# The hidden layer of an MLP in groups of four 128-column blocks instead of two, behind a top-k attention

## The chip, the cores and the metric

The kernel runs on one core of a Trainium2 chip. The time is the device time of one execution in microseconds (us), the median over runs; lower is better. Five engines work side by side, each through its own queue in order: TensorE (PE in the profile; its weight loads are PEld), VectorE (DVE), ScalarE (ACT), GpSimd (POOL), and SyncE (SP), which issues the DMAs.

## The reference

```python
# top-k attention, q, k, v: (8, 8, 576, 64) float32, top_k = 32
scores = scale * np.matmul(q, k.transpose(0, 1, 3, 2))
kth = np.partition(scores, -top_k, axis=-1)[..., -top_k:-top_k + 1]
scores = np.where(scores >= kth, scores, -1000000000.0)
scores = scores - np.max(scores, axis=-1, keepdims=True)
attn = np.exp(scores)
attn = attn / (np.sum(attn, axis=-1, keepdims=True) + 1e-09)
x = np.matmul(attn, v)          # then (B, H, S, D) -> (4608, 512)
# MLP, w_in: (512, 2048), w_out: (2048, 512)
h = x @ w_in
g = np.where(h >= 1, h, np.where(h <= -1, 0.0, (h + 1) ** 2 / 4))
out = g @ w_out
```

The kernel computes g as min(relu(0.5 h + 0.5), 1) squared, plus relu(h - 1).

## The kernel before, in words

**Attention.** The work is cut into 144 steps. A step m is one tile of 128 query rows (of one of 8 batches) for a pair of heads. A step consists of:

- `scores` (L285, L287): PE writes the scores `sp` of 128x576 for each of two heads into PSUM, and ACT copies them to `s`.
- `first_top` (L300 to L323): DVE makes `more`, the pairwise maximum of two halves of the scores, and the first eight maxima; ACT takes `nmax` and the exponentials `e` of both heads. DVE's L300 also makes `less`, the pairwise minimum, for the step before.
- `weights` (L348 to L386): DVE finds the 32 largest with rounds of eight maxima and a match_replace, then the threshold `kth`, and L386 masks `e` and sums it to `z`.
- `divide` (L332, L339, L342): DVE takes 1/z as `rz`; POOL multiplies `e` by it, one instruction a head, and records `excess`, a number for a check at the end.
- `move_w` (L416 to L419): ACT splits `e` into 16-bit `halves`, one instruction a head; SP writes them to DRAM as `rows` and fetches them back transposed as `wT`.
- `values` (L433, L441, L446): PE multiplies `wT` with the values into `po`, and ACT copies this into the tile's `xT`.

DVE's loop over a step is long, so the stages of several steps are interleaved. With step m running on DVE, the scores of step m+2 and the values of step m-2 are issued at slot 4 of seven; the division of step m-1 stands at slot 0 and its `halves` at slot 2.

**MLP.** Four steps complete one chunk of 128 tokens, 36 chunks in all. `mlp` then queues that chunk's work. `hidden(x)` multiplies `w_in` with `xT` for GROUP = 2 blocks of 128 hidden columns into one PSUM tile `ph` (L466). ACT reads it twice (L470 gives `r`, L477 gives `g`), and POOL finishes with a clamp, a square and a sum (L482, L483, L484). `final(f)` accumulates block f times `w_out` into `py` (L489), and after the 16th block ACT copies `py` to `y` and SP stores it. A final comes LAG = 4 groups behind its hidden group. The last chunk uses groups of one block and lets DVE and ACT do POOL's part.

**Order.** Nothing reorders at run time: the order of each engine's instructions is written down by the builder. `mlp` appends to `pending`, first in first out; `advance` runs after each of the seven slots and takes units off while their cost (128-column passes of PE: `NK * group` for a hidden group, four for a final) fits the amount that is due by then. The amount is spread evenly over the remaining steps. Every instruction of a unit, on PE, ACT and POOL, enters the engines' order at that point:

```python
pending.append((NK * group, needed(x * group + group - 1, False), partial(hidden, x), False))
...
if due < cost or pe_time >= until:
    break
```

**Early stage.** In the first 13 or so steps the two weight matrices arrive as 64 pieces of 64-bit words and are converted by ACT, DVE and POOL (`convert_piece`). A hidden group can be queued only when all its blocks' pieces are there. In this stage the division and the transpose of `e` are done by PE (`transpose_w`) instead of POOL, `halves` and DMA. From then on, every second step ACT also runs two `sign` instructions (L168) that inspect a weight piece.

**PSUM and SBUF.** `ph` and `po` share three PSUM banks; `sp`, `pq`, `pk` and `pw` share two double banks; `py` has one. `r` has 2 buffers, `g` has 2 * LAG, `y` has 2.

Of the kernel before, what the change touches and what calls it, by code (L numbers as in the profile page):

```python
# [10 lines left out]
F32 = mybir.dt.float32  # L11
# [4 lines left out]
ALU = mybir.AluOpType  # L16
# [8 lines left out]
def kernel(  # L25
# [10 lines left out]
    nc = tc.nc  # L36
    B, H, S, D = q.shape
    NTOK, DM = out.shape
    DFF = moe_w_in.shape[1]
    P = 128  # L40
# [10 lines left out]
    BANK = 512  # L51
    NK = DM // P
    NF = DFF // P
    GROUP = 2
    LAG = 4
    SCALE = float(D) ** -0.5

    const = ctx.enter_context(tc.tile_pool(name="const", bufs=1))
# [42 lines left out]
    n_pieces = NK * DFF // WC + NF * DM // WC  # L101
# [12 lines left out]
    def needed(f, second):  # L114

        return (f // n_in) * (NK + n_in * n_out) + NK + (n_out * (f % n_in + 1) if second else 0)
# [55 lines left out]
    def run(ctx, paired):  # L172
# [284 lines left out]
        def mlp(xT, rows, pool, last):  # L457
            gs, group = {}, 1 if last else GROUP
            py = []

            def hidden(x):
                ph = ps.tile([P, group, P], F32, name="ph", tag="ph", bufs=3)
                for i in range(group):
                    f = x * group + i
                    for kk in range(NK):
                        nc.tensor.matmul(ph[:, i], w_in[:, kk, f * P:(f + 1) * P], xT[:, kk],  # L466
                                         start=(kk == 0), stop=(kk == NK - 1))

                r = pool.tile([P, GROUP, P], F32, name="r", bufs=2)[:, 0:group]
                nc.scalar.activation(r, ph, AF.Relu, bias=half, scale=0.5)  # L470
                gs[x] = g = pool.tile([P, GROUP, P], F32, name="g", bufs=2 * LAG)[:, 0:group]
                if last:
                    nc.vector.tensor_scalar(g, ph, -1.0, 0.0, ALU.add, ALU.max)
                    nc.scalar.activation(r, r, AF.Square)
                    nc.vector.scalar_tensor_tensor(out=g, in0=r, scalar=1.0, in1=g, op0=ALU.min, op1=ALU.add)
                    return
                nc.scalar.activation(g, ph, AF.Relu, bias=minus, scale=1.0)  # L477
                if converted < n_pieces and x % 2:
                    nc.scalar.activation(r, r, AF.Square)
                    nc.gpsimd.tensor_scalar(r, r, 1.0, 0.0, ALU.min, ALU.max)  # L480
                else:
                    nc.gpsimd.tensor_scalar(r, r, 1.0, 0.0, ALU.min, ALU.max)  # L482
                    nc.gpsimd.tensor_tensor(out=r, in0=r, in1=r, op=ALU.mult)  # L483
                nc.gpsimd.tensor_tensor(out=g, in0=r, in1=g, op=ALU.add)  # L484

            def final(f):
                if f == 0:
                    py.append(ps.tile([P, DM], F32, name="py", tag="py", bufs=1))
                nc.tensor.matmul(py[0], gs[f // group][:, f % group], w_out[:, f, :], start=(f == 0), stop=(f == NF - 1))  # L489
                if f == NF - 1:  # L490
                    y = (late or words).tile([P, DM], F32, name="y", bufs=2)
                    nc.scalar.copy(y, py[0])  # L492
                    for p0, p1, dst in rows:
                        nc.sync.dma_start(out=dst, in_=y[p0:p1])

            behind = []
            while pending and pending[-1][3]:
                behind.insert(0, pending.pop())  # L500
            for x in range(NF // group + LAG):
                if x < NF // group:
                    pending.append((NK * group, needed(x * group + group - 1, False), partial(hidden, x), False))
                if x < LAG:
                    for _ in range(min(GROUP, len(behind))):
                        pending.append(behind.pop(0)[0:3] + (False,))
                else:
                    for f in range((x - LAG) * group, (x - LAG + 1) * group):
                        pending.append((DM // P, needed(f, True), partial(final, f), x >= NF // group))
# [3 lines left out]
        for b in range(0, B, 2):  # L513
            a, c, tl = [(b, t) for t in range(NT)], [(b + 1, t) for t in range(NT)], (b, NT)
# [15 lines left out]
        words, late = conversion.enter_context(tc.tile_pool(name="words", bufs=1)), None  # L530
        pending = deque()
        total, spent = len(chunks) * (NK * NF + NF * DM // P), 0
        converted, inspected, due = 0, 0, 0.0
# [127 lines left out]
        for m in range(n + 2):  # L661
# [3 lines left out]
            elif not early and late is None:  # L665
                conversion.close()
                late = ctx.enter_context(tc.tile_pool(name="late", bufs=1))
# [108 lines left out]
```

## Time and profile before

| what | us |
|---|---|
| runs (3): lowest, median, highest | 1607.3, 1609.65, 1610.31 |
| the profiled execution, its own time | 1610.32 |
| its span in the trace | 1608.5 |
| PE busy | 1514.0 (94%) |
| DVE busy | 1422.1 (88%) |
| ACT busy | 1140.4 (71%) |
| POOL busy | 943.3 (59%) |
| ACT reading `ph`: L470 and L477, 280 each of 128x256 | 133.1 and 131.8 |
| POOL's L482, L483, L484 | 150.7, 201.5, 219.6 |

Times in the profile are in us from the span's start. A row of the timeline gives start, duration, engine, source line, operation, the tiles written and read, shapes and a count; a bracket at its end gives the engine's idle time before it and what ended that. A row of the waits gives the waiting instruction, what it waited for, the total, the number of times and the longest. PE's ends are modelled, so PE's busy time is an upper estimate of what it did.

### The profile page before, as it was taken

Reading aid. Unit: us, or ns where it says so; the run is one execution under the profiler, and the core shown is the slowest. Engines: PE = TensorE matmul, PEld = TensorE weight load, DVE = VectorE, ACT = ScalarE, POOL = GpSimd, SP = SyncE. Lnnn points to the kernel's source line nnn. Section 1 sums busy time; section 2 is a strip of 40 time slices with the busy share of each in tenths; the row PEclk is TensorE's granted clock in tenths of the full one; section 3 lists DMA queues with packets and bytes.
Section 4 is the critical chain, followed back from the end, with each engine's and each line's share of the span. In section 5 each row is a group of like instructions: output and inputs, shape, how many; then the busy total and the mean of one; then the engine's idle time right before and its main releaser. Section 6 shows DMA issues by size and latency. Waiting matters only on the chain.

```text
span 1608.5 us, 32395 instructions
## 1 busy us (share of the span) xinstructions
PE 1514.0 (94%) x10925; PEld 1080.7 (67%) x10925; DVE 1422.1 (88%) x4443; ACT 1140.4 (71%) x2308; POOL 943.3 (59%) x1376
## 2 busy tenths in 40 slices
PE   5587999999999999999999999999999999999988
PEld 4465676777667776777667767766666667666665
DVE  7999889999998998999999998999898998889932
ACT  5677567777777767777768877776677776677632
POOL 5766466666555665655556666555555665556640
PEclk7798999999999999999999999999999999999999
DMA  9433246565465556665565545655565555544410
GB/s 252 132 96 110 72 130 174 157 158 153 133 174 161 154 143 173 161 150 145 145 172 159 160 133 157 172 143 140 135 174 146 142 142 130 145 131 126 123 51 16
DMA packets 439056, 227.92 MB, mean 142 GB/s; under 512 B 393056, under 2 KB 401248, under 8 KB 438880
## 3 DMA queue, kind: packets, MB, share of 16 engines
q1 hardware_dynamic: 438880, 225.75, 51.8%
q8 instruction: 88, 1.44, 0.4%
q14 instruction: 88, 0.72, 0.1%
HBM read 62.91 MB, written 86.11 MB: 93 GB/s over the span
## 4 chain that ended last, share of the span: by engine, by line
PE 71%; ACT 13%; POOL 4%; DVE 4%; DMA 4%; issue 3%; SPq 1%; POOLq 0%; ACTq 0%; DVEq 0%
PE ph L466 27%; PE py L489 24%; PE sp L285 8%; PE po L433 7%; ACT halves L416 3%; ACT e L323 3%; DMA wT<-rows 2%; ACT s L287 2%; ACT sign L168 2%; PE pw L401 1%; POOL e L339 1%; POOL r L483 1%; PE po L441 1%; ACT r L470 1%; POOL g L484 1%
## 5 line engine op out<-in xcount | busy, mean ns | idle before, releaser
L466 PEld LDWEIGHTS ph<-xT,w_in 128*128 128x128 f32 x4608 | 554.4, 192 | 118.3 <-issue 79.8
L466 PE MATMUL ph<-xT,w_in 128*128 128x128 f32 x4608 | 576.1, 278 | 14.8 <-ACT xT L446 12.9
L489 PE MATMUL py<-w_out,g 128*128 128x512 f32 x1152 | 558.6, 601 | 7.3 <-ACT y L492 7.1
L482 POOL TENSOR_SCALAR r<-r 128x256 f32<-128x256 f32 x276 | 150.7, 546 | 526.5 <-ACT r L470 526.1
L307 DVE MATCH_REPLACE8 more<-tops,more 128x288 f32<-128x288 f32 x864 | 375.2, 437 | 0.0
L416 ACT COPY halves<-e 128x1152 uint16<-128x1152 uint16 x260 | 288.0, 1153 | 112.7 <-POOL e L339 111.5
L470 ACT ACTIVATE r<-ph,half 128x256 f32<-128x256 f32 (+1 forms) x296 | 139.0, 470 | 241.1 <-PE ph L466 227.9
L489 PEld LDWEIGHTS py<-w_out,g 128*128 128x128 f32 x1152 | 193.5, 191 | 137.0 <-issue 131.2
L386 DVE SCALAR_TENSOR_TENSOR e<-s,kth,e 128x577 f32<-128x577 f32 x288 | 249.2, 900 | 0.1
L484 POOL TENSOR_TENSOR g<-r,g 128x256 f32<-128x256 f32 x280 | 219.6, 784 | 22.0
L323 ACT ACTIVATE e<-s,nmax 128x576 f32<-128x576 f32 x288 | 217.4, 770 | 4.7
L339 POOL TENSOR_SCALAR e<-e,rz 128x576 f32<-128x576 f32 x260 | 218.6, 851 | 0.0
L483 POOL TENSOR_TENSOR r<-r 128x256 f32<-128x256 f32 x276 | 201.5, 730 | 23.0
L300 DVE TENSOR_TENSOR more<-s 128x576 f32<-128x576 f32 x144 | 114.9, 798 | 109.0 <-ACT s L287 108.6
L287 ACT ACTIVATE s<-sp 128x576 f32<-128x576 f32 x288 | 169.2, 638 | 4.5 <-PE sp L285 4.2
L285 PE MATMUL sp<-kT,qT 64*128 64x288 f32 x1024 | 162.0, 433 | 9.9 <-ACT kT L244 9.0
L285 PEld LDWEIGHTS sp<-kT,qT 64*128 64x128 f32 x1024 | 89.6, 188 | 98.9 <-issue 29.1
L433 PE MATMUL po<-wT,v_in 128*64 128x128 f32 x2048 | 145.9, 282 | 10.3 <-DMA wT<-rows 7.9
L433 PEld LDWEIGHTS po<-wT,v_in 128*64 128x64 f32 x2048 | 113.4, 139 | 60.5 <-issue 37.5
L477 ACT ACTIVATE g<-ph,minus 128x256 f32<-128x256 f32 x280 | 131.8, 471 | 0.0
L348 DVE MAX8 tops<-more 128x8 f32<-128x288 f32 x288 | 125.4, 442 | 0.0
L300 DVE TENSOR_TENSOR less<-s 128x576 f32<-128x576 f32 x144 | 117.4, 815 | 0.0
(92 smaller groups left out, 1528.2 us busy)
## 6 DMA issues: line engine op xcount, KB each, us to landing
rows<-halves SPq DMA_DIRECT2D x130, 576.0 KB, 2.8
raw<-in_moe_w_out_dram SPq DMA_DIRECT2D x52, 256.0 KB, 2.8
raw<-in_moe_w_in_dram SPq DMA_DIRECT2D x48, 256.0 KB, 2.9
k_in<-in_k_dram SPq DMA_DIRECT2D x64, 128.0 KB, 3.2
q_in<-in_q_dram SPq DMA_DIRECT2D x32, 256.0 KB, 3.3
v_in<-in_v_dram SPq DMA_DIRECT2D x8, 1024.0 KB, 5.9
out_dram<-y SPq DMA_DIRECT2D x32, 256.0 KB, 3.0
kT<-in_moe_w_in_dram SPq DMA_DIRECT2D x16, 256.0 KB, 4.6
```

Of the source, the lines that this page charges most:

```text
L285: nc.tensor.matmul(o[:, a0 - c0:a1 - c0], qT[d, g, :], kT[d, g, k0:k0 + a1 - a0], start=True, stop=True)
L300: nc.vector.tensor_tensor(out=x, in0=s[:, :, 0:SH], in1=s[:, :, SH:S], op=op)
L307: nc.vector.match_replace(out=st["rest"][:, i, :], in_to_replace=eight(st["tops"], i, r - 8), in_values=src[:, i, :], imm_value=LOWEST)
L323: nc.scalar.activation(e[:, i, :], s[:, i, :], AF.Exp, bias=nmax[:, i:i + 1])
L339: nc.gpsimd.tensor_scalar(st["e"][:, i, :], st["e"][:, i, :], rz[:, i:i + 1], 1.0, ALU.mult, ALU.mult)
L386: nc.vector.scalar_tensor_tensor(out=st["all"][1][:, i, :], in0=st["all"][0][:, i, :], scalar=last[i], in1=st["all"][1][:, i, :], op0=ALU. ...
L416: nc.scalar.copy(halves[:, :, i * S:(i + 1) * S], st["e"][:, i, :].bitcast(U16).rearrange("p (k t) -> p t k", t=2))
L433: nc.tensor.matmul(po[j * D:(j + 1) * D], v_in[:, h, c, :] if c < NT else v_tl[0][:, h, :], wT[:, block(j, c)], start=(c == 0), stop=(c == ...
L466: nc.tensor.matmul(ph[:, i], w_in[:, kk, f * P:(f + 1) * P], xT[:, kk], start=(kk == 0), stop=(kk == NK - 1))
L483: nc.gpsimd.tensor_tensor(out=r, in0=r, in1=r, op=ALU.mult)
L484: nc.gpsimd.tensor_tensor(out=g, in0=r, in1=g, op=ALU.add)
L489: nc.tensor.matmul(py[0], gs[f // group][:, f % group], w_out[:, f, :], start=(f == 0), stop=(f == NF - 1))
```

## The change

GROUP becomes 4 and LAG becomes 2, so the distance between a block's hidden and final products stays eight blocks for all chunks but the last, where groups are of one block and the distance falls from four blocks to two. `ph` then fills a whole PSUM bank with 128x512. ACT reads it with two instructions of 512 columns. POOL's three operations stay at 256 columns: they are issued for the first two blocks, then for the last two. The cost that `advance` compares with the due amount is `NK * group`, so a hidden unit costs 16 instead of 8 and is taken off half as often. `r` grows with GROUP; `g` keeps its size (half as many buffers, twice as large); `y` has one buffer instead of two.

```diff
-    GROUP = 2
-    LAG = 4
+    GROUP = 4
+    LAG = 2
...
                 nc.scalar.activation(g, ph, AF.Relu, bias=minus, scale=1.0)
-                if converted < n_pieces and x % 2:
+                squared = converted < n_pieces and x % 2
+                if squared:
                     nc.scalar.activation(r, r, AF.Square)
-                    nc.gpsimd.tensor_scalar(r, r, 1.0, 0.0, ALU.min, ALU.max)
-                else:
-                    nc.gpsimd.tensor_scalar(r, r, 1.0, 0.0, ALU.min, ALU.max)
-                    nc.gpsimd.tensor_tensor(out=r, in0=r, in1=r, op=ALU.mult)
-                nc.gpsimd.tensor_tensor(out=g, in0=r, in1=g, op=ALU.add)
+                for c in range(0, group, 2):
+                    rh, gh = r[:, c:c + 2], g[:, c:c + 2]
+                    nc.gpsimd.tensor_scalar(rh, rh, 1.0, 0.0, ALU.min, ALU.max)
+                    if not squared:
+                        nc.gpsimd.tensor_tensor(out=rh, in0=rh, in1=rh, op=ALU.mult)
+                    nc.gpsimd.tensor_tensor(out=gh, in0=rh, in1=gh, op=ALU.add)
...
-                    y = (late or words).tile([P, DM], F32, name="y", bufs=2)
+                    y = (late or words).tile([P, DM], F32, name="y", bufs=1)
```

## The prediction, made before the changed kernel had run

> **What bounds the kernel now.** I read the page's busy shares first, then the total waits, then one step of the timeline on ACT and on POOL, and last the order of instructions in the two built programs, which holds no times.
>
> ```profile
> PE 1514.0 (94%) x10925; PEld 1080.7 (67%) x10925; DVE 1422.1 (88%) x4443; ACT 1140.4 (71%) x2308; POOL 943.3 (59%) x1376
> POOL r L482 <- ACT r L470: 526.1, 201, 9.0
> ACT r L470 <- PE ph L466: 227.9, 155, 3.5
> ACT halves L416 <- POOL e L339: 111.5, 59, 3.5
> DVE more L300 <- ACT s L287: 108.6, 89, 4.9
> ```
>
> PE is nearly full, and its few stalls after 200 us add up to about 30 us (it waits for `xT` 14.8, for `wT` some 10, for `y` 7.1). By the shares, ACT and POOL have room to spare. The waits say otherwise: ACT waits for POOL's `e`, and POOL waits for ACT's `r`. That is a ring. ACT's queue runs `halves` of one step, then everything up to `r`; POOL's queue runs the three operations on `r`, then `e`; and `e` releases the next `halves`. Here is one turn on ACT, then the part on POOL that closes it:
>
> ```profile
> 778.46 2.21 ACT L416 COPY halves<-e 128x1152 uint16<-128x1152 uint16 x2 [2.80 <-POOL e L339]
> 780.57 0.47 ACT L470 ACTIVATE r<-ph,half 128x256 f32<-128x256 f32 x1
> 780.94 0.46 ACT L477 ACTIVATE g<-ph,minus 128x256 f32<-128x256 f32 x1
> 781.29 0.20 ACT L321 ACTIVATE nmax<-tops 128x2 f32<-128x2 f32 x1
> 781.52 1.44 ACT L323 ACTIVATE e<-s,nmax 128x576 f32<-128x576 f32 x2
> 782.87 1.17 ACT L287 ACTIVATE s<-sp 128x576 f32<-128x576 f32 x2
> 783.93 0.26 ACT L446 COPY xT<-po 128x128 f32<-128x128 f32 x1
> 784.08 0.49 ACT L470 ACTIVATE r<-ph,half 128x256 f32<-128x256 f32 x1
> 784.45 0.49 ACT L477 ACTIVATE g<-ph,minus 128x256 f32<-128x256 f32 x1
> 788.17 2.21 ACT L416 COPY halves<-e 128x1152 uint16<-128x1152 uint16 x2 [3.23 <-POOL e L339]
> ```
>
> ```profile
> 784.67 1.24 POOL L482 TENSOR_SCALAR r<-r 128x256 f32<-128x256 f32 x1 [1.63 <-ACT r L470]
> 785.99 0.61 POOL L483 TENSOR_TENSOR r<-r 128x256 f32<-128x256 f32 x1
> 786.68 0.72 POOL L484 TENSOR_TENSOR g<-r,g 128x256 f32<-128x256 f32 x1
> 787.38 1.50 POOL L339 TENSOR_SCALAR e<-e,rz 128x576 f32<-128x576 f32 x2
> ```
>
> In this turn neither `r` waits for PE. The time from `halves` to `halves`, 9.71 us, is the sum of the queue: ACT 5.62 to the second `r`, 0.59 until POOL starts, 2.71 for three operations, 0.79 for the first `e`. The next turn, which holds the two `sign` instructions, takes 10.45 us (778.46, 788.17, 798.62). PE's work in such a step is 9.62 us (scores at 777.46 and at 787.08). So PE and the ring run almost level. The mean over all 129 turns of the trace is 10.40 us.
>
> **ScalarE's two reads.** 280 instructions of 475 ns and 280 of 471 ns become 140 pairs of 512 columns. No such row exists; the ACT copy `y` of 128x512 from PSUM takes 587 ns, and the line through `r` at 128 columns (367) and 256 (475) gives 690. I take 0.6, nearest to the copy. ACT's busy time falls by 265 - 280 x 0.6 = 97 us. That is worth nothing by itself: in the ring only what stands before `r`'s end counts, and there one early pair of `r` and `g` goes (0.72 us in the turn shown) and the remaining `r` grows by 0.13.
>
> **GpSimd: the same operations, at another place.** Count and size stay. What moves is which of them stand between `r` and `e`. Before, each turn holds two hidden groups. One has its three operations done while ACT is at `e` and `s`; only the other is in the ring. Now each turn holds one group of four blocks, all six operations come from one `r`, and where that `r` is the last thing before `halves`, all six stand ahead of `e`. I matched POOL's order with ACT's in the changed program, for each of 129 turns: are all POOL operations of the hidden groups that ACT has read before `halves` queued ahead of this `halves`' `e`, and does ACT read `ph` after `s`? Both hold in 66 turns (35 without `sign`, 31 with), mostly in three stretches of about 20. In 30 turns POOL's six are ahead, but ACT reads `ph` early, among `nmax` and `e`; in 33 the six are queued behind `e`. Those 63 leave the ring slack.
>
> **The sum for a tight turn.** ACT from `halves` to `r`: 5.62 - 0.72 = 4.90. From `r` to POOL's start 0.57 (mean where POOL was idle), plus 0.13 for the wider read: 0.70. POOL's three operations ahead of an `e` take 2.24 us on the mean of 128 (1.88 to 3.19), twice: 4.48. `e` until `halves` starts: 0.88 (mean; 0.79 above). Total 10.96 us, with `sign` 1.17 more (791.92 to 793.09): 12.13. So 35 x 10.96 + 31 x 12.13 = 760 us where 66 x 10.40 = 686 stood: **+74 us**. Bounds: six operations at the least seen, 2 x 1.88, with 0.66 and 0.78 at their ends, give +17; at the 2.71 of the turn above they give +126. I stay at the mean, because one POOL group will meet DVE's two-input L300 (the 1.24 above, against 0.40 elsewhere) and the other will not: 2.71 + 1.88 = 4.59.
>
> GPSIMD Engine Reference of the Trainium skill, section 8, says that GpSimd shares its SBUF interfaces with VectorE and contends with instructions that have two SBUF inputs; this speaks against queueing more POOL work in the ring. The trace agrees in those 1.24 against 0.40 us. By that rule alone, all six slowed, the sum would go to the upper bound.
>
> **PE.** Same matmuls. In a tight turn PE has 9.6 to 10.1 us of work in 11.5, so it idles some 1.4 us. It will sit before `po`, since `wT` lands about 8.0 us after `halves` ends (780.67 to 788.64 here, where PE waited 0.32). In the 63 other turns PE sets the pace as now. The first final of a chunk now follows four hidden blocks (3.56 us) after the old chunk's last final, not two (1.78), so the 7.1 us of waiting for `y` goes: -6. One buffer for `y` costs nothing, as its stores lie some 40 us apart, against 3.0 to land.
>
> **Early stage.** By the order, PE has 16 units of 0.22 us less MLP work behind it at steps 9 to 31, as groups wait for four blocks' pieces: 4 us put off. DVE fills this stage (40.00 of 40 us in 40:80), and the tight stretches have idle PE to take it: 0, at most +4. **Tail.** After the second to last `pw`, 224 units remain in both programs. In the last chunk a block's final comes two blocks behind: 3.5 us on PE against 1.3 from its `ph` to DVE's `g`. 0.
>
> **Total:** the profiled execution took 1610.3 (the median of three is 1609.65, so it is used as it is); 1610.3 + 74 - 6 = 1678.
>
> **Rivals.**
> - *PE paces everywhere and its stalls shrink (faster).* The ring stays slack because POOL's six are done in time. It decides at 10.40 - 4.90 - 0.70 - 0.88 - 0.55 (`sign`'s share) = 3.37 us for six operations; the least seen for two groups is 3.76. Then 7 us of `y` and half of the 14.8 us for `xT` go: 1610.3 - 14 = 1596. For it: POOL's 59% share and ACT's 97 us of relief.
> - *PE paces, and the only effect is the early 4 us and coarser units:* 1610 to 1616. For it: a few us of slack at the start of each stretch. Against: 20 turns in a row use that up.
> - *The ring is worse than summed:* beyond 1736, with the slow POOL price in every turn or the 30 early turns bound as well (their sum: 9.0, and 10.2 with `sign`).
> - *PE's clock falls because of the pauses.* The window 80:120, PE busy 34.54 of 40, has a clock of 0.91; at that, 10.0 us of work becomes 11.0, still under 11.5. TensorE: Matmul & The Clock Gate, Part 1, has the clock fall only after an idle window of some 3.4 us; the pauses summed here are shorter.
>
> **How the numbers follow.** The ring between its bounds, 1620 to 1736: 0.70. Faster: 0.10. PE-paced, 1607 to 1616: 0.12, of which 0.04 is within 0.2% (3.2 us, about what a measurement can tell from no change). Worse than 1736: 0.08. The range 1618 to 1728 leaves out the faster rival and the upper end.
>
> **What would show it.** Right: ACT `halves` waiting for POOL `e` for 300 to 400 us in all; ACT's wait for `ph` down by half; DVE's wait for `s` up by some 70; PE waiting for `wT` 60 to 100; tight turns at 11 and 12 us in alternation, early ones at 10. Wrong: `halves` to `halves` at 10.4 or less where `r` stands last, or PE above 96% busy in 250 to 500 us.

## The result, and the profile after

The changed kernel takes 1751.16 us (median of four runs, 1748.58 to 1752.12) against 1608.47 us before: 1.0884 times as long, 95% interval 1.0865 to 1.0903. The direction was forecast, the size was not: 1678 us with a range of 1618 to 1728.

The page's busy shares and five rows of the total waits (us in total, times, longest), of the changed kernel:

```profile
PE 1556.6 (89%) x10925; PEld 1113.8 (64%) x10925; DVE 1452.5 (83%) x4443; ACT 1094.5 (63%) x2026; POOL 940.0 (54%) x1376
POOL r L483 <- ACT r L470: 657.4, 138, 12.4
ACT halves L416 <- POOL e L339: 325.8, 86, 5.0
DVE more L300 <- ACT s L287: 218.8, 94, 7.4
PE po L433 <- DMA wT<-rows: 72.7, 38, 4.6
PE ph L466 <- ACT xT L446: 29.2, 9, 5.6
```

No engine got more instructions. ACT is busy 46 us less, POOL about as long; PE and DVE are busy 43 and 30 us longer with the same instructions, for which see below (the clock, and DVE's L386). Every engine's share fell, and the waits between ACT and POOL grew: `halves` for `e` from 111.5 to 325.8 us. PE now waits for `wT`, which `halves` feeds (from 7.9 to 72.7).

One tight turn of the ring, the timeline on ACT and then on POOL:

```profile
396.63 2.37 ACT L416 COPY halves<-e 128x1152 uint16<-128x1152 uint16 x2 [5.03 <-POOL e L339]
398.91 0.20 ACT L321 ACTIVATE nmax<-tops 128x2 f32<-128x2 f32 x1
399.14 1.44 ACT L323 ACTIVATE e<-s,nmax 128x576 f32<-128x576 f32 x2
400.49 1.17 ACT L287 ACTIVATE s<-sp 128x576 f32<-128x576 f32 x2
401.55 0.26 ACT L446 COPY xT<-po 128x128 f32<-128x128 f32 x1
401.70 0.71 ACT L470 ACTIVATE r<-ph,half 128x512 f32<-128x512 f32 x1
402.28 0.70 ACT L477 ACTIVATE g<-ph,minus 128x512 f32<-128x512 f32 x1
408.00 2.37 ACT L416 COPY halves<-e 128x1152 uint16<-128x1152 uint16 x2 [5.02 <-POOL e L339]
```

```profile
402.49 0.88 POOL L483 TENSOR_SCALAR r<-r 128x256 f32<-128x256 f32 x1 [4.51 <-ACT r L470]
403.46 0.61 POOL L485 TENSOR_TENSOR r<-r 128x256 f32<-128x256 f32 x1
404.15 0.72 POOL L486 TENSOR_TENSOR g<-r,g 128x256 f32<-128x256 f32 x1
404.84 0.40 POOL L483 TENSOR_SCALAR r<-r 128x256 f32<-128x256 f32 x1
405.32 0.61 POOL L485 TENSOR_TENSOR r<-r 128x256 f32<-128x256 f32 x1
406.01 0.72 POOL L486 TENSOR_TENSOR g<-r,g 128x256 f32<-128x256 f32 x1
406.72 2.46 POOL L339 TENSOR_SCALAR e<-e,rz 128x576 f32<-128x576 f32 x2
```

Between 402.98 and 408.00 ACT stands still: the six POOL operations, but for the first half microsecond, and the first `e` lie in that gap. The turn is 11.37 us; with `sign` it is 12.5.

The 140.9 us by which the span grew (1608.5 to 1749.4), by class of turn, each against 10.40 us, the mean turn before:

| stretch | after, us | before, us | difference |
|---|---|---|---|
| ahead of the first `halves` | 195.0 | 190.6 | +4.4 |
| 66 tight turns | 832.6 | 686.5 | +146.1 |
| of these: 54 at 12.03, 12 of 13.3 to 17.8 | 649.4, 183.2 | 561.7, 124.8 | +87.7, +58.4 |
| 30 turns with the early `r` | 295.0 | 312.0 | -17.0 |
| 33 turns with POOL's work behind `e` | 352.8 | 343.2 | +9.6 |
| behind the last turn | 74.1 | 76.2 | -2.1 |

The classes are those of the prediction, made from the order of instructions before the kernel ran. The tight ones hold the whole loss. The turns with the same numbers in the trace of before say the same: the 66 took 677.5 us there (now +155.1), the 30 took 312.7 (-17.7), the 33 took 351.6 (+1.2).

### The profile page after: what moved, and what is told of

Its sections match the earlier page's. It is cut to its first block, busy times and chain, and to the rows that moved or that the text cites. A ratio compares the mean times of both kernels' runs of the same rounds, so it can differ in the third digit from the quotient of the medians.

```text
span 1749.4 us, 31719 instructions
## 1 busy us (share of the span) xinstructions
PE 1556.6 (89%) x10925; PEld 1113.8 (64%) x10925; DVE 1452.5 (83%) x4443; ACT 1094.5 (63%) x2026; POOL 940.0 (54%) x1376
## 4 chain that ended last, share of the span: by engine, by line
PE 48%; ACT 20%; POOL 19%; DVE 5%; DMA 4%; issue 4%; POOLq 0%; SPq 0%; ACTq 0%; DVEq 0%
PE ph L466 20%; PE py L491 15%; POOL e L339 7%; PE po L433 5%; PE sp L285 5%; ACT e L323 5%; POOL g L486 5%; ACT halves L416 4%; POOL r L485 4%; ACT s L287 4%; POOL r L483 3%; DMA wT<-rows 2%; ACT sign L168 2%; ACT r L470 2%; PE pw L401 1%
## 5 line engine op out<-in xcount | busy, mean ns | idle before, releaser
L466 PE MATMUL ph<-xT,w_in 128*128 128x128 f32 x4608 | 580.5, 286 | 33.0 <-ACT xT L446 29.2
L466 PEld LDWEIGHTS ph<-xT,w_in 128*128 128x128 f32 x4608 | 560.1, 200 | 75.7 <-issue 35.0
L491 PE MATMUL py<-w_out,g 128*128 128x512 f32 x1152 | 538.9, 600 | 2.2 <-ACT y L494 1.8
L416 ACT COPY halves<-e 128x1152 uint16<-128x1152 uint16 x260 | 292.0, 1153 | 329.6 <-POOL e L339 325.8
L491 PEld LDWEIGHTS py<-w_out,g 128*128 128x128 f32 x1152 | 202.8, 191 | 186.1 <-issue 179.3
L300 DVE TENSOR_TENSOR more<-s 128x576 f32<-128x576 f32 x144 | 114.9, 798 | 219.2 <-ACT s L287 218.8
L386 DVE SCALAR_TENSOR_TENSOR e<-s,kth,e 128x577 f32<-128x577 f32 x288 | 275.1, 991 | 0.1
L339 POOL TENSOR_SCALAR e<-e,rz 128x576 f32<-128x576 f32 x260 | 268.0, 1039 | 8.5 <-DVE rz L332 8.4
L470 ACT ACTIVATE r<-ph,half 128x512 f32<-128x512 f32 (+1 forms) x156 | 102.7, 658 | 208.5 <-PE ph L466 208.1
L433 PE MATMUL po<-wT,v_in 128*64 128x128 f32 x2048 | 152.7, 291 | 76.1 <-DMA wT<-rows 72.7
L485 POOL TENSOR_TENSOR r<-r 128x256 f32<-128x256 f32 x276 | 190.1, 689 | 23.0
L433 PEld LDWEIGHTS po<-wT,v_in 128*64 128x64 f32 x2048 | 118.1, 143 | 128.8 <-DMA wT<-rows 87.8
L348 DVE MAX8 tops<-more 128x8 f32<-128x288 f32 x288 | 125.5, 443 | 0.0
L300 DVE TENSOR_TENSOR less<-s 128x576 f32<-128x576 f32 x144 | 118.3, 821 | 0.0
L320 DVE MAX8 tops<-more 128x8 f32<-128x288 f32 x288 | 116.8, 446 | 0.0
```

Of the source, the lines that this page charges most:

```text
L339: nc.gpsimd.tensor_scalar(st["e"][:, i, :], st["e"][:, i, :], rz[:, i:i + 1], 1.0, ALU.mult, ALU.mult)
L386: nc.vector.scalar_tensor_tensor(out=st["all"][1][:, i, :], in0=st["all"][0][:, i, :], scalar=last[i], in1=st["all"][1][:, i, :], op0=ALU. ...
L416: nc.scalar.copy(halves[:, :, i * S:(i + 1) * S], st["e"][:, i, :].bitcast(U16).rearrange("p (k t) -> p t k", t=2))
L433: nc.tensor.matmul(po[j * D:(j + 1) * D], v_in[:, h, c, :] if c < NT else v_tl[0][:, h, :], wT[:, block(j, c)], start=(c == 0), stop=(c == ...
L485: nc.gpsimd.tensor_tensor(out=rh, in0=rh, in1=rh, op=ALU.mult)
```

## The experiments

Theory 1 is the ring. Theory 2 is that the loss comes from the coarse units on PE, the wide ACT reads, or the pauses and the clock they cost. All runs are timed beside the kernel before on the same chip, whose median was 1608.7 to 1611.4 us.

**1. GpSimd's part behind the next division, in the changed kernel.** The six operations go into a list that is emptied at the end of `divide`, or ahead of the next hidden group or of a final that needs them.

```diff
+            def finish(r, g, squared, group):
+                for c in range(0, group, 2):
+                    ...
             def hidden(x):
+                flush()
...
-                for c in range(0, group, 2):
-                    ...
+                held.append((gs, x, partial(finish, r, g, squared, group)))
...
         def divide(st):
+            divide_only(st)
+            flush()
```

> The changed kernel, with one thing moved: GpSimd's six operations of a hidden group are queued behind the next division (after both e instructions) instead of ahead of it. Same instructions, same TensorE and ScalarE order. Theory 1 (the ring halves - r - six GpSimd operations - e - halves sets the tight turns): the ring opens in all turns, TensorE paces at 9.8 to 10.4 us a turn, time 1590 to 1625; ScalarE's wait of halves for e falls from 326 us to under 60. Theory 2 (the loss comes from coarser units on TensorE, the wide ScalarE reads or the pauses and the clock they cost, whatever GpSimd's order): 1735 to 1755.

Measured: 1594.43 us, 0.9902 of the kernel before (0.9886 to 0.9919), 157 us below the changed kernel. ACT's wait of `halves` for `e` is gone from its waits. The timeline of one turn, on POOL and on ACT (lines are shifted by the edit):

```profile
388.91 0.73 POOL L477 TENSOR_TENSOR g<-r,g 128x256 f32<-128x256 f32 x1
391.55 1.47 POOL L349 TENSOR_SCALAR e<-e,rz 128x576 f32<-128x576 f32 x2 [1.91 <-DVE rz L342]
394.73 1.08 POOL L474 TENSOR_SCALAR r<-r 128x256 f32<-128x256 f32 x1 [1.55 <-ACT r L489]
...
393.95 0.69 ACT L489 ACTIVATE r<-ph,half 128x512 f32<-128x512 f32 x1 [3.45 <-PE ph L485]
398.31 2.21 ACT L426 COPY halves<-e 128x1152 uint16<-128x1152 uint16 x2
```

POOL now waits for DVE's `rz`, does `e` at once, and takes the hidden group afterwards. `e` is ready at 393 and `halves` starts at 398 with no wait. ACT waits for PE instead, as it should where PE sets the pace. Theory 2 falls: the same coarse units, wide reads and final distance are in this kernel.

**2. The ring's content, not GpSimd's load: one operation left out.** `L485`, the multiply, is dropped.

> The changed kernel without L485, GpSimd's multiply of r by itself (its output is therefore not the reference's). Two of the six operations leave each hidden group, about 2 x 0.69 us. Theory 1: each of the 66 tight turns gets 1.3 to 1.4 us shorter, 12.0 to 10.7 us, time 1651 to 1671. Theory 2: GpSimd is busy 54% of the span, so taking work from it moves nothing: 1740 to 1755.

Measured: 1643.43 us, 108 us below the changed kernel where 80 to 100 was expected. The stretch from the first operation to `e` fell from 4.23 to 2.87 us (means over tight turns in which `r` did not wait for PE), and, unforeseen, `e` to `halves` from 1.28 to 0.79.

**3. ScalarE reads 256 columns at a time, in the changed kernel.**

```diff
+                for c in range(0, group, 2):
+                    nc.scalar.activation(rh, ph[:, c:c + 2], AF.Relu, bias=half, scale=0.5)
+                    nc.scalar.activation(gh, ph[:, c:c + 2], AF.Relu, bias=minus, scale=1.0)
```

> The changed kernel with ScalarE reading the bank 256 columns at a time (r, g, three GpSimd operations for the first two blocks, then the same for the last two). TensorE's order stays. Theory 1: GpSimd starts 0.2 us earlier in a tight turn, its six operations still stand ahead of e: 66 x 0.2 = 13 us off, 1730 to 1745. Theory 2 in the form that the wide reads hold ScalarE up: 1620 to 1680.

Measured: 1734.98 us, 16 below the changed kernel and inside the band of theory 1, but not by POOL's earlier start alone. In the 43 tight turns in which `r` does not wait for PE, POOL starts 0.59 us after `r` instead of 0.80, and `e` to `halves` takes 0.78 us instead of 1.28: such a turn is 0.8 us shorter. Yet 19 tight turns instead of 12 are above 13.2 us, and in each of them `r` waits for PE, which takes most of this back. The wide reads are not the cause of the loss: experiment 1 keeps them.

**4. The same move in the kernel before.**

> The kernel before, with the same move of GpSimd's operations behind the next division (at most one hidden group held at a time). Theory 1: 54 of 129 turns of the kernel before are tight at about 10.1 us, where TensorE has 9.6 to 10.0 us of work: 5 to 20 us off, 1588 to 1603. Theory 2 (TensorE alone paces the kernel before): 1605 to 1611.

Measured: 1589.91 us, 0.9874 of before (0.9857 to 0.9890). The kernel before was itself held by the ring in part of its turns: `halves` waited 111.5 us for `e`, and with the edit of experiment 1 this wait is gone.

**5. A chunk's MLP work queued one step later, in the changed kernel.** Twelve tight turns were long, and in all of them `r` waits for PE. Here is the longest but one, the timeline on PE and on ACT, then two windows of the same turn (PE, PEld, DVE, ACT and POOL busy, granted clock, DMA share, GB/s):

```profile
1464.83 0.94 PE L466 MATMUL ph<-xT,w_in 128*128 128x128 f32 x6
1470.90 5.92 PE L466 MATMUL ph<-xT,w_in 128*128 128x128 f32 x26 [5.13 <-ACT xT L446]
...
1464.51 2.37 ACT L416 COPY halves<-e 128x1152 uint16<-128x1152 uint16 x2 [4.55 <-POOL e L339]
1470.59 0.26 ACT L446 COPY xT<-po 128x128 f32<-128x128 f32 x1
1476.85 0.69 ACT L470 ACTIVATE r<-ph,half 128x512 f32<-128x512 f32 x1 [6.01 <-PE ph L466]
1482.17 2.21 ACT L416 COPY halves<-e 128x1152 uint16<-128x1152 uint16 x2 [4.05 <-POOL e L339]
```

```profile
1464.00:1471.00 7.00, 1.87 (x25) 1.51 (x20) 4.59 (x16) 6.20 (x12) 1.86 (x3) 0.93 0.34 117
1471.00:1477.00 6.00, 6.00 (x27) 5.89 (x28) 6.00 (x18) 0.15 (x1) 0.00 (x0) 0.52 0.48 107
```

The group is the first of a new chunk and reads the `xT` of the step just finished. Its copy stands on ACT behind `halves`, which waits for POOL's `e`. So PE pauses 5.13 us, loses half its clock, and then 26 of the group's 32 passes at that clock (5.92 us) stand between `xT` and `r`: PE has joined the ring, and the turn takes 17.66 us.

Only four of the twelve are of this kind. Six are like the next one, in which PE is idle nowhere and its clock is full (the timeline on PE, then on ACT):

```profile
1296.67 3.84 PE L466 MATMUL ph<-xT,w_in 128*128 128x128 f32 x32
1292.08 2.20 ACT L416 COPY halves<-e 128x1152 uint16<-128x1152 uint16 x2
1300.54 0.69 ACT L470 ACTIVATE r<-ph,half 128x512 f32<-128x512 f32 x1 [3.46 <-PE ph L466]
1306.74 2.21 ACT L416 COPY halves<-e 128x1152 uint16<-128x1152 uint16 x2 [4.32 <-POOL e L339]
```

It is the first tight turn behind a slack one, as are all six. The `halves` that opens it had not waited for `e` (no bracket in its row): ACT and POOL had run ahead of PE, and now `r` waits for PE's whole group of four blocks before POOL's six operations can start.

The edit starts a chunk's work with the values of the next step:

```diff
-                    mlp(xTs[ch], rows_of(*chunks[ch]), mlp_pool, ch == len(chunks) - 1)
+                    arrived.append(ready[valued])   # started with the next step's values
```

> The changed kernel, with each chunk's MLP work queued one step later, so that the first hidden group of a chunk no longer follows directly on the chunk's last values on TensorE. By the order of instructions 59 turns are tight instead of 66. Theory 1b (the 12 long tight turns of 13.3 to 17.8 us come from TensorE waiting for xT at a chunk's start, which puts xT's place in ScalarE's queue and the whole hidden group into the ring): they fall to 12.0 us, and with the seven fewer tight turns 59 x 12.0 + 70 x 10.1 = 1415 us stand where 1480 stood: 1680 to 1705. Rival (the long turns come from the short backlog and the coarse units late in the run, whatever chunk starts): only the seven turns count, 1730 to 1745.

Measured: 1710.57 us, 41 us below the changed kernel, of which about 13 are the seven tight turns fewer (an estimate: 12.0 against 10.1 us each). That is between the two expectations: PE's wait for `xT` is gone altogether (29.2 us before this edit), but 19 of the 59 tight turns are still above 13 us. In 13 of these 19 the turn before had ended with a `halves` that did not wait for `e`, some of those turns only 6 to 7 us long, as in the second kind. The chunk's start is a real part of the long turns, not all of them.

**6. GpSimd on 512 columns, in the changed kernel.** This undoes "GpSimd keeps 256 columns an operation".

> The changed kernel with GpSimd's three operations on 512 columns instead of twice three on 256, undoing the part of the change that keeps them at 256. ScalarE and TensorE orders stay. Theory 1: the stretch from the first operation to e shrinks from 4.23 us to what three wide operations take, an estimate of 2.9 to 3.5 us from the 0.48 us spacing at 256 and 0.74 at 576 for the one-input operation and one to two times the 0.69 for the two-input ones: 66 x 0.7 to 1.3 us off, 1665 to 1705. If the time per column dominates (twice the 256 price), no change: 1740 to 1755.

Measured: 1678.62 us, 73 us below the changed kernel. The groups on POOL (columns: shapes, count, busy and mean ns):

```profile
L484 POOL TENSOR_TENSOR g<-r,g 128x512 f32<-128x512 f32 x140 | 183.5, 1311 | 11.0
L483 POOL TENSOR_TENSOR r<-r 128x512 f32<-128x512 f32 x138 | 148.4, 1076 | 11.5
```

An operation of twice the width takes 1.6 times as long (1076 against 689 ns, 1311 against 791), so the stretch ahead of `e` is 3.53 us instead of 4.23. Here too `e` to `halves` falls from 1.28 to 0.78.

**7. Half of the group's work behind the division.** Three operations stay ahead of `e`, three are held.

> The changed kernel with only the second half of each hidden group's GpSimd work (three of six operations, two blocks) queued behind the next division; the first half stays ahead of e. A point between the changed kernel (six ahead: 4.23 us from the first operation to e) and the full move (none ahead). Theory 1: with three ahead, 5.60 + 0.80 + 2.1 + 0.8 = 9.3 us on the mean of a tight turn, below TensorE's 10.1, so the ring is open as in the full move: 1590 to 1615. If the loss goes with the amount of GpSimd work ahead of e without a point from which it decides, about half of the 157 us comes back: 1660 to 1685.

Measured: 1621.09 us, six us above the band of theory 1 and 39 below the other. With the runs above there are five points for the work ahead of `e`: 4.23 us gives 1751, 3.53 gives 1679, 2.87 gives 1643, 2.34 gives 1621, none gives 1594. In the first step `e` to `halves` falls with it, so the stretch from POOL's first operation to `halves` is the fairer measure: its three steps (1.20, 0.65 and 0.49 us) bring 60, 54 and 46 us for each us, and the last 2.34 us of work ahead of `e` only 11. So the price falls off towards PE's turn without a sharp point. Experiment 3 lies off this line, with 16 us for 0.8 us a regular turn. That turns with `sign` are bound longer than those without may be why; this was not tested.

**8. and 9. Both moves together,** in the kernel before and in the changed one.

> The kernel before with GpSimd's operations behind the next division (1589.9 us) and each chunk's work queued one step later. With the ring open only TensorE's waits for xT (6.9 us) are left to gain: 1582 to 1592. A step of lag at the end may cost as much: up to 1596.

> The changed kernel with GpSimd's operations behind the next division (1594.4 us) and each chunk's work queued one step later. Theory 1b: without GpSimd in the ring the chunk's start costs TensorE only the 5.9 us of waits for xT that are left: 1587 to 1597. If a chunk's start were slow by itself, some 40 us would come off here as in the run without the move: 1550 to 1560.

Measured: 1575.64 us (0.9794 of before, 0.9765 to 0.9822) and 1586.88 us (0.9870, 0.9832 to 0.9908). With the ring open a later chunk start saves the changed kernel 7.5 us, not 41, so most of its price came through the ring. The kernel before with both moves is faster than both kernels; its busy shares:

```profile
PE 1501.1 (95%) x10925; PEld 1072.6 (68%) x10925; DVE 1426.9 (91%) x4443; ACT 1140.1 (72%) x2308; POOL 906.8 (58%) x1376
```

It gained 14 us by the later start where at most 8 were expected. The traces place 8 of them in the 129 turns (1320.1 to 1311.7 us) and 5 ahead of the first `halves` (189.8 to 184.6), which the expectation had left out. And with both moves the change of group size still costs 11 us: not in the turns, whose sum is the same (1311.0 against 1311.7), but ahead of the first `halves` (193.7 against 184.6) and behind the last turn (79.5 against 77.0). Why the early stage differs by 9 us and not by 4 is open.

## Why the prediction was right and wrong

**Right: the mechanism and its place.** The 66 turns called tight are the slow ones, the 30 early ones even gained (9.83 us a turn), and ACT's wait for `e` came out at 326 us (300 to 400 said), PE's for `wT` at 73 (60 to 100). Two of the signs were off: DVE's wait for `s` grew by 110, not 70, and ACT's wait for `ph` hardly fell (227.9 to 208.1); 42 us of the latter lie in the twelve long turns, and 105 in the 33 turns with POOL's work behind `e`. Experiments 1, 2 and 7 are three sizes of one cause.

**The tight turn: nearly right, 0.5 us short.** Means over the 47 tight turns in which `r` did not wait for PE:

| part | said, with `sign`'s share | measured |
|---|---|---|
| `halves` to `r` on ACT | 5.45 | 5.66 |
| `r` to POOL's start | 0.70 | 0.80 |
| six operations to `e` | 4.48 | 4.23 |
| `e` to `halves` | 0.88 | 1.28 |

The term that was most off is the last. The prediction let one POOL group collide with DVE's L300 and took `e` at its mean; but the longer ring moves `e` onto DVE's other two-input operation, the mask L386. The pair of `e` that opens the turn shown, and DVE at that time:

```profile
395.35 2.46 POOL L339 TENSOR_SCALAR e<-e,rz 128x576 f32<-128x576 f32 x2
394.96 1.03 DVE L386 SCALAR_TENSOR_TENSOR e<-s,kth,e 128x577 f32<-128x577 f32 x1
395.92 1.29 DVE L386 SCALAR_TENSOR_TENSOR e<-s,kth,e 128x577 f32<-128x577 f32 x1
```

Both are slowed: two `e` take 2.46 us instead of 1.47, and L386 1.03 and 1.29 instead of 0.81. Over the whole trace, the 105 `e` that overlap L386 take 1.24 us each on the mean, and 0.74 is the usual time; L386 takes 1.16 beside `e` and 0.81 alone. In experiment 2 `e` falls mostly ahead of L386 and takes 1.47 a pair again, which is where its unforeseen gain came from. In all, 54 tight turns were 0.51 us longer than the 11.52 forecast: 27 of the 73 us that were missing, some 21 of them by this term.

**The step that failed: in a tight turn PE "has 9.6 to 10.1 us of work in 11.5, so it idles some 1.4 us".** PE was taken to be ahead of the ring in every tight turn, and the sum held no turn in which `r` waits for PE. In twelve turns it does, by 0.8 to 6.3 us: 183.2 us instead of 12 x 11.52, 45 of the missing 73 us. They are of three kinds:

- Four, 22 of the 45 us, are the chunk starts of experiment 5: PE waited 3.9 to 5.7 us for `xT`, and its clock in the turn was 0.79 to 0.81.
- Six, 19 us, are the first tight turns behind a slack one, at full clock and without a pause of PE: `halves` had run ahead of PE, and the turn had to wait for both.
- Two, 4 us, follow a wait of PE for `wT` of 3.38 and 4.60 us, at a clock of 0.81 and 0.87.

For the first kind the rows were there: the trace of before has ten waits of `ph` for `xT`, 12.9 us, and the order of the changed program shows where a new chunk's group follows its own values. They were booked as a gain ("half of the 14.8 us for `xT` go", in the rival); in a closed ring they are a loss, as `xT` itself comes late. For the second, the prediction knew that the tight turns come in stretches, but its sum priced the first of a stretch like the others.

The rest balances: the other 63 turns came to -7.4 (-6 said), the early stage to +4.4 (at most +4 said), the tail to -2.1 (0 said).

**The clock: wrong, with little harm in most turns.** The prediction excluded a drop, as the pauses summed were under the 3.4 us that TensorE: Matmul & The Clock Gate, Part 1, of the Trainium skill gives for an idle window. The trace does not agree. PE paused 2.21 us ahead of 370.4, and the clock fell there (windows, columns as above):

```profile
360.00:370.00 10.00, 8.17 (x48) 5.43 (x47) 7.59 (x25) 7.37 (x14) 4.13 (x7) 1.00 0.52 145
370.00:380.00 10.00, 9.61 (x63) 7.80 (x64) 8.74 (x27) 6.25 (x10) 5.28 (x7) 0.83 0.20 72
```

In regular turns PE's slack hides it: the turn from 408.00 had a clock of 0.86 and took 12.54 us like its neighbours. In six of the long turns the clock was 0.79 to 0.87, and there the slow passes stand in the ring.

**The rivals.** The faster one needed the six operations in 3.37 us; they took 4.23. Its argument, POOL's idle share, is refuted by experiment 2: less work on an engine that is busy 54% of the time gave 108 us. The rival above 1736 had the time right, but for neither of its reasons: the six operations took 4.23 us, not the slow price, and the early turns gained. It was the slowed `e` and the long turns. (Its bound of 1736 leaves out the 6 us for `y`; with them the sum's upper end is 1730.) **Small terms:** the wait for `y` fell from 7.1 to 1.8 us as said; the wide read took 0.69 us, not 0.6, which makes the saving 72 us instead of 97; ACT's busy time fell by 46 only, as ACT's instructions overlap in the trace (each starts before the one ahead of it has ended) and the 265 us counted the overlap twice.

## What to carry to other kernels

Two in-order queues that wait for each other form a ring, and its turn is the sum of what stands between the two waits, however idle both engines look; add up that sum before merging instructions, and look where the order puts the release. Moving the release ahead of the bulk work, with the instructions unchanged, was worth 157 us here and 21 in the kernel before. And when a ring closes, ask for every engine that was ahead of it whether it stays ahead in the worst turn, not in the mean one.

## What the hardware showed unexpectedly

- PE's granted clock went to 0.5 for 3.4 to 6.8 us around pauses of 2.21, 2.96, 2.97, 2.55 and 2.86 us (between 370 and 492 us of the changed kernel); over 300 to 480 us, where the longest pause is 3.59, its mean was 0.95. The length of a pause alone does not decide: the clock stayed at 1.0 around one of 3.01 us at 942.7, and in the kernel before around one of 3.52 at 822.2.
- POOL's two-input operations cost 1.6 times as much at twice the width (689 to 1076 ns, 791 to 1311 ns).
- POOL's `e` and DVE's L386 slow each other (0.74 to 1.24 us and 0.81 to 1.16 on the means). In the changed kernel DVE waits for ACT's `s` 94 times, so it turns with the ring, and in its regular tight turns `e` meets the same L386 in every turn and not now and then (`e` to `halves` 1.28 on the mean, 1.29 at most).
